# Ten small MLP chunks instead of two, one unit transposed on TensorE instead of four, and early score groups moved from units 26, 62, 98 to 62, 98, 134

## Chip, cores and metric

The kernel runs on one core of one Trainium2 chip. The metric is the device time of one execution in microseconds (us). The median of three runs before the change is 1459.1 us (1457.85 to 1459.69).

## The reference, cut to what matters

Top-32 attention for 8 batches, 8 heads, 576 tokens and head width 64, then a two-layer MLP with a leaky ReLU over all 4608 tokens. Everything is float32.

```
scores = (1/8) * q @ k^T                       # per batch and head, 576 x 576
kth    = 32nd largest score of each row
attn   = softmax of the scores >= kth, others masked out
x      = (attn @ v), heads side by side        # 4608 tokens x 512
h      = x @ w_in                              # 512 -> 2048
out    = max(0.01*h, h) @ w_out                # 2048 -> 512
```

## The kernel before, in words

**Units.** Attention is cut into 144 units (L209 to L216). A whole unit is 128 query rows of two heads (a pair), so four units make 128 tokens complete in all eight heads. 576 is not a multiple of 128, so each batch also has two units that take the 64 rows left over from two pairs each. Even batches have them at the end, odd ones at the start: units 16 to 19, 52 to 55 and so on. Each batch has 18 units.

**A unit's way through the engines.** TensorE makes its scores (`scores`, L218, for two units at once), ScalarE copies them to `s_sb` (L242). VectorE finds the 32 largest of each row (`top_k`, L299; its first instruction for a unit is the TENSOR_TENSOR of L306). GpSimd masks (L324, L325), ScalarE exponentiates (L328) and copies the sums (`ze`, L333), VectorE takes reciprocals (`rz`, L337), ScalarE normalises (L340). Then the weights are transposed: ScalarE splits them into 16-bit halves (L349), SyncE sends these to DRAM (L350) and brings them back transposed (`wT`, L354). The units named in `HASTY` are instead transposed by nine TensorE instructions and two ScalarE copies (L364, L370). TensorE multiplies with v (L393 for two whole units, L405 for left-over units), and ScalarE copies the values to `x` (`keep_values`, L412 to L417).

**The order.** It is written out by hand: the loop over slots at L618 runs `top_k` of unit s in slot s, masks unit s-1, and normalises and transposes unit s-2. In even slots it issues the scores of units s+2 and s+3. The values of a pair of units are issued at the place that `values_at` (L490) gives: for units under 14 in the middle of slot (n|1)+4, later at the end of slot (n|1)+3, and one slot earlier for the units in `HURRIED`. All engines run their own instructions in this order, so an instruction that waits holds back what stands behind it on its engine.

**The MLP.** `CHUNKS` (L54) cuts the 4608 tokens into chunks of 128 or 256. When the values of a chunk's last units have been issued, the chunk is ready. `mlp` (L425) is a generator. Per chunk, 64 matmuls (L436) with the chunk's tokens as moving columns make h, 8 Prelu copies for 256 tokens or 4 for 128 (L442; each covers 512 columns) make `gT`, and 16 matmuls of 512 columns (L448) for each 128 tokens make the output. In the trace each of these float32 matmuls is two records. `x` has two buffers, so chunk c+2 writes where chunk c was read.

**How much MLP in which slot.** `mlp_steps(budget)` is called seven times a slot and issues MLP matmuls until the budget, counted in columns, is used. `slot_budget` (L518) sets it. While at most two chunks have become ready it is `EARLY_SHARE` = 500 per call, 3500 columns a slot. After that, all columns that are ready and not yet issued are spread evenly over the slots up to the next chunk's due slot:

```
        if len(after) >= len(CHUNKS) - EARLY:
            return EARLY_SHARE
        return backlog[0] / ((until + 1 - s) * SLOTS)
```

A chunk of 256 counts as 64 x 256 + 32 x 512 = 32768 columns, one of 128 as 64 x 140 + 16 x 512 = 17152 (`COLUMNS`, L423).

**Early scores.** For a in `KEPT` (L498), the scores of units a, a+1, a+8 and a+9 are made in slots 0 to 5 (`keep_scores`, L277, the matmuls of L286), kept in DRAM, and fetched three slots before they are used (L297). Their slots then have no score matmuls.

Of the kernel before, what the change touches and what calls it, by code (L numbers as in the profile page):

```python
# [20 lines left out]
def kernel(  # L21
# [29 lines left out]
    WCH = 1024  # L51
    LEFT = S % P
    assert D == 64 and S == 576 and HP == 4 and B % 2 == 0 and LEFT == 64
    CHUNKS = [128] * 2 + [256] * 17  # L54
    assert sum(CHUNKS) == B * S
    CHMAX = max(CHUNKS)
    LOADED, LOADED_V = 5, 5
# [260 lines left out]
    def mask(u, i):  # L318
        if i == 0:
            u.nbias = small.tile([P, 2], F32, name="nbias")  # L320
            u.z = small.tile([P, 2], F32, name="z")
            nc.gpsimd.tensor_scalar(u.nbias, u.tops[:, :, 0, 0], -SCALE, None, ALU.mult)
        pen = work.tile([P, S], F32, name="pen", bufs=1)
        nc.gpsimd.tensor_scalar(pen, u.s[i], u.tops[:, i, ROUNDS - 1, 7:8], MASKED, ALU.is_lt, ALU.mult)  # L324
        nc.gpsimd.tensor_tensor(u.s[i], u.s[i], pen, ALU.add)  # L325
# [16 lines left out]
    def transpose(u, between):  # L342


        pairs = u.both.rearrange("p i n -> p (i n)").bitcast(U16).rearrange("p (n h) -> p n h", h=2)
        apart = halves.tile([P, 2, 2 * S], U16, name="apart")
        for h in range(2):
            split = work.tile([P, 2 * S], U16, name="split", bufs=2)
            nc.scalar.copy(split, pairs[:, :, h])  # L349
            nc.sync.dma_start(apart[:, h, :], split)  # L350
            if h == 0:
                between()
        u.wT = work.tile([P, 2 * NKC - 1, P], F32, name="wT", bufs=3)
        nc.sync.dma_start_transpose(out=u.wT.bitcast(U16), in_=apart.rearrange("p h n -> (p h) n"))  # L354

    def transpose_in_haste(u):

        both = u.both.rearrange("p i n -> p (i n)")
        u.parts_T = []
        for c0, c1 in ((0, 8), (8, 2 * NKC - 1)):  # L360
            pt = ps_sc.tile([P, 2, 512], F32, name="wide", bufs=2)
            pt = pt.rearrange("p h (c n) -> p (h c) n", n=P)
            for c in range(c0, c1):
                nc.tensor.transpose(pt[:, c - c0, :], both[:, c * P:(c + 1) * P], ident)  # L364
            u.parts_T.append((c0, c1, pt))

    def keep_transposed(u):
        u.wT = work.tile([P, 2 * NKC - 1, P], F32, name="wT", bufs=3)
        for c0, c1, pt in u.parts_T:
            nc.scalar.copy(u.wT[:, c0:c1, :], pt[:, 0:c1 - c0, :])  # L370

    x_of = {}

    def x_at(token):

        c = 0
        while token >= CHUNKS[c]:
            token -= CHUNKS[c]  # L380
            c += 1
        return c, token
# [29 lines left out]
    def keep_values(pair, po, b, q0):  # L412
        ch, col = x_at(b * S + q0)
        if ch not in x_of:
            x_of[ch] = [xpool.tile([P, CHMAX], F32, name=f"x{c}") for c in range(HP)]
        for side in range(2):
            nc.scalar.copy(x_of[ch][pair % HP + side][:, col:col + po.shape[-1]], po[:, side, :])  # L417
# [7 lines left out]
    def mlp(ch):  # L425

        n = CHUNKS[ch]
        t0 = sum(CHUNKS[:ch])
        x = x_of[ch]
        span = 2 * CHMAX // n  # L430
        for f0 in range(0, NFC, span):
            ph = ps_ml.tile([P, span, n], F32, name="ph", tag="ml")
            for i in range(span):
                f = f0 + i
                for c in range(HP):
                    nc.tensor.matmul(  # L436
                        ph[:, i, :], w_in[c][:, f * P:(f + 1) * P], x[c][:, 0:n],
                        start=(c == 0), stop=(c == HP - 1),
                    )
                    if c == HP - 1 and i + 1 < span or c == 1 and n == CHMAX:  # L440
                        yield COLUMNS[n] * (4 if n < CHMAX else 2)
            nc.scalar.activation(gT[:, f0:f0 + span, 0:n], ph, AF.Prelu, alpha=SLOPE)  # L442
            yield COLUMNS[n] * (4 if n < CHMAX else 2)
        for r0 in range(0, n, P):
            m = min(P, n - r0)
            pz = ps_ml.tile([P, 512], F32, name="pz", tag="ml")
            for f in range(NFC):
                nc.tensor.matmul(  # L448
                    pz[0:m, 0:DMODEL], gT[:, f, r0:r0 + m], w_out[f // 4][:, f % 4, :],
                    start=(f == 0), stop=(f == NFC - 1),  # L450
                )
                if f % 2 and f + 1 < NFC:
                    yield 2 * DMODEL
            o_sb = work.tile([P, DMODEL], F32, name="o_sb", bufs=1)
            nc.scalar.copy(o_sb[0:m], pz[0:m, 0:DMODEL])  # L455
            nc.sync.dma_start(out[t0 + r0:t0 + r0 + m, :], o_sb[0:m])
            yield 2 * DMODEL
# [8 lines left out]
    def mlp_steps(budget):  # L466
        owed[0] += budget
        while owed[0] > 0:
            if running[0] is None:
                if not ready:  # L470
                    owed[0] = 0.0
                    return
                running[0] = mlp(ready.pop(0))
            cost = next(running[0], None)
            if cost is None:
                running[0] = None
            else:
                owed[0] -= cost
                backlog[0] -= cost
# [2 lines left out]

    LAG = 3
    HURRY = 20
    HURRIED = (15, 23, 31)
    HASTY = (14, 15, 23, 31)
    UNHURRIED = 14
    MIDDLE, END = 0, 1

    def values_at(n):  # L490

        if n < UNHURRIED:
            return (n | 1) + LAG + 1, MIDDLE
        return (n | 1) + LAG - ((n | 1) in HURRIED), END

    steps = units

    KEPT = (26, 62, 98)  # L498
    EARLY_SCORES = {0: 4, 1: 2, 2: 1, 3: 2, 4: 1, 5: 2}

    def unit(n):
# [3 lines left out]
    for n, u in enumerate(steps):  # L505
        ch, _ = x_at(u.b * S + u.q0)
# [22 lines left out]
    with tc.manual_schedule():  # L529
        last = {p: n for n, u in enumerate(steps) for p in u.pairs}  # L530
        starts = {p: n for n, u in reversed(list(enumerate(steps))) for p in u.pairs}

        to_keep = [[steps[n] for n in (a, a + 1, a + 8, a + 9)] for a in KEPT]
        early_units = {u for us in to_keep for u in us}
# [60 lines left out]
        def weights_of(u):  # L595
            reciprocals(u)
            normalize(u, 0)
            normalize(u, 1)

        def values(*place):  # L600
            due = [u for n, u in enumerate(steps) if values_at(n) == place]
            if not due:
                return ()
            po = ps_sc.tile([P, 2, 512], F32, name="wide", bufs=2)
            if len(due[0].pairs) == 1:
                weigh_whole(due, po, FULL + [NKC - 1] if place[1] == MIDDLE else
                            [QUARTERS] + FULL if place[0] < HURRY else FULL + [QUARTERS])
                return [(due[0], po[:, :, 0:P])]
            for n, u in enumerate(due):
                weigh_left(u, po[:, :, n * LEFT:(n + 1) * LEFT])  # L610
            return [(u, po[:, :, n * LEFT:(n + 1) * LEFT]) for n, u in enumerate(due)]

        def keep(weighed, *place):
            for u, po in weighed:
                keep_values(u.pairs[0], po, u.b, u.q0)
            attended(*place)

        for s in range(len(steps) + LAG + 1):  # L618
# [9 lines left out]

            at_first = s < HURRY and s - 2 in HURRIED
            if at_first:  # L630
                weights_of(older)
            slot()
            if old:
                mask(old, 0)
                mask(old, 1)
            late = s < HURRY and not {s - 1, s - 2} & set(HURRIED)
            if older and not late and not at_first:
                weights_of(older)
            mlp_steps(budget)
            weighed = values(s, MIDDLE)  # L640
            at_once = s - 2 in HASTY or any(at == (s, MIDDLE) for at, _ in ready_at)
            if at_once:
                keep(weighed, s, MIDDLE)
            slot()
            if older and late:
                weights_of(older)
            if s - 2 in HASTY:
                transpose_in_haste(older)
# [4 lines left out]
            if older:  # L653
                keep_transposed(older) if s - 2 in HASTY else transpose(older, lambda: mlp_steps(budget))
            if not older or s - 2 in HASTY:
                mlp_steps(budget)
# [84 lines left out]
```

## Time and profile before

| | us |
|---|---|
| median of the runs | 1459.1 |
| the profiled execution | 1455.5 |
| its span, first to last instruction | 1453.5 |
| TensorE (PE) matmul busy | 1393.5 |
| VectorE (DVE) busy | 1320.2 |
| ScalarE (ACT) / GpSimd (POOL) busy | 1096.7 / 1099.2 |

The profiled execution lies 3.6 us under the median and has 2 us outside the span. PE means the matmuls, PEld the loads of their stationary operand; the ends of matmuls are modelled, so a PE that is shown busy need not be at its peak. The 40 slices of the page are 36.3 us each; a digit is the busy share in tenths. In a timeline each line has the start, the duration, the engine, the line of the kernel, output<-input, the shape and the number of records, and in brackets the idle time before with what ended it.

"Slot s of DVE" below begins with the first L306 of unit s; "slot s of PE" begins with the first TensorE instruction that the program issues in slot s. The records of PE stand in the program's order, so counting them against the loop tells which slot each belongs to.

### The profile page before, as it was taken

The numbers are of one execution on the slowest core, as the hardware profiler recorded it, in microseconds if no ns is written. First come the engines' busy times: TensorE is split into PE (matmuls) and PEld (weight loads), VectorE is DVE, ScalarE is ACT, GpSimd is POOL, SyncE is SP. The second block draws the span as 40 slices with busy tenths as digits, with TensorE's granted clock in tenths as the row PEclk, the third lists the DMA queues.
The fourth block names the chain that finished last, engine by engine and source line by source line (L and its number), as shares of the span: only waits on it lengthen the run. The fifth ranks groups of instructions, "written<-read, shape, count | busy, mean of one in ns | idle before, by whom it ended". The sixth has DMA issues, their size and how long they took to land.

```text
span 1453.5 us, 26353 instructions
## 1 busy us (share of the span) xinstructions
PE 1393.5 (96%) x9140; PEld 917.4 (63%) x9140; DVE 1320.2 (91%) x3401; ACT 1096.7 (75%) x1976; POOL 1099.2 (76%) x744
## 2 busy tenths in 40 slices
PE   7848999999999999999999999999999999999998
PEld 2326667575756676757676667666666666666674
DVE  7999999999999999999999999999999999999600
ACT  8878777777887787777778778777778777878710
POOL 3288887888888888788888878888888887788600
PEclk9968999999999999999999999999999999999999
DMA  8967542756676645667566644676766654554510
GB/s 331 339 218 229 139 122 83 195 157 164 155 180 172 164 138 156 175 185 179 163 174 170 171 138 134 176 194 163 185 163 185 162 150 120 172 141 133 152 40 15
DMA packets 394998, 239.17 MB, mean 165 GB/s; under 512 B 334576, under 2 KB 336112, under 8 KB 392944
## 3 DMA queue, kind: packets, MB, share of 16 engines
q1 hardware_dynamic: 394864, 237.48, 58.9%
q8 instruction: 72, 1.18, 0.3%
q14 instruction: 62, 0.51, 0.1%
HBM read 55.77 MB, written 99.09 MB: 107 GB/s over the span
## 4 chain that ended last, share of the span: by engine, by line
PE 65%; DVE 24%; DMA 4%; ACT 4%; issue 2%; POOL 0%; DVEq 0%; SPq 0%; ACTq 0%; POOLq 0%
PE ph L436 25%; PE pz L448 25%; DVE tops L311 11%; DVE pairs L314 8%; PE wide L393 8%; PE wide L235 4%; DMA wT<-apart 3%; DVE pairs L306 2%; PE narrow L235 2%; PE wide L405 1%; ACT split L349 1%; ACT s_sb L340 1%; DMA apart<-split 1%; DMA raw<-in_weights_dram 1%; ACT s_sb L328 1%
## 5 line engine op out<-in xcount | busy, mean ns | idle before, releaser
L324 POOL TENSOR_SCALAR pen<-s_sb,tops 128x576 f32<-128x576 f32 x288 | 638.7, 2218 | 194.7 <-DVE tops L311 126.9
L311 DVE MAX8 tops<-pairs 128x8 f32<-128x288 f32 (+1 forms) x1152 | 635.7, 591 | 0.0
L436 PE MATMUL ph<-x,w_in 128*128 128x256 f32 (+1 forms) x2432 | 514.5, 371 | 2.7 <-ACT gT L442 2.7
L448 PE MATMUL pz<-w_out,gT 128*128 128x512 f32 x1152 | 504.4, 594 | 0.0
L436 PEld LDWEIGHTS ph<-x,w_in 128*128 128x128 f32 x2432 | 439.0, 190 | 84.1 <-issue 25.4
L314 DVE MATCH_REPLACE8 pairs<-tops,pairs 128x288 f32<-128x288 f32 (+1 forms) x864 | 460.1, 538 | 0.0
L325 POOL TENSOR_TENSOR s_sb<-s_sb,pen 128x576 f32<-128x576 f32 x288 | 407.7, 1415 | 24.0
L448 PEld LDWEIGHTS pz<-w_out,gT 128*128 128x128 f32 x1152 | 216.5, 190 | 264.9 <-issue 262.1
L349 ACT COPY split<-s_sb 128x1152 uint16<-128x1152 uint16 x280 | 309.5, 1146 | 0.0
L340 ACT ACTIVATE s_sb<-s_sb,rz 128x576 f32<-128x576 f32 x288 | 207.5, 772 | 56.8 <-DVE rz L337 56.6
L328 ACT ACTIVATE s_sb<-s_sb,nbias 128x576 f32<-128x576 f32 x288 | 222.1, 771 | 7.8 <-POOL s_sb L325 7.8
L306 DVE TENSOR_TENSOR pairs<-s_sb 128x576 f32<-128x576 f32 x288 | 214.8, 784 | 9.8 <-DVE tops L311 0.5
L393 PE MATMUL wide<-wT,vt 128*64 128x128 f32 (+1 forms) x2560 | 159.5, 284 | 15.5 <-DMA wT<-apart 7.1
L393 PEld LDWEIGHTS wide<-wT,vt 128*64 128x64 f32 (+1 forms) x2560 | 132.0, 138 | 62.8 <-issue 39.6
L442 ACT ACTIVATE gT<-ph 128x512 f32<-128x512 f32 x144 | 85.4, 593 | 55.9 <-PE ph L436 55.7
L417 ACT COPY x<-wide 128x128 f32<-128x128 f32 (+1 forms) x160 | 32.2, 260 | 114.2 <-PE wide L393 102.2
L242 ACT COPY s_sb<-wide 128x704 f32<-128x704 f32 x130 | 98.2, 755 | 8.4 <-PE wide L235 2.6
L455 ACT COPY o_sb<-pz 128x512 f32<-128x512 f32 x36 | 21.1, 585 | 90.4 <-PE pz L448 90.4
L235 PE MATMUL wide<-kt,qt 64*64 64x352 f32 x704 | 72.6, 475 | 1.0 <-ACT s_sb L257 0.7
L242 ACT COPY s_sb<-narrow 128x448 f32<-128x448 f32 x130 | 63.0, 538 | 0.5
L314 DVE MATCH_VALUE_LOAD pairs<-tops,pairs 128x8 f32 x864 | 62.4, 72 | 0.0
L328 ACT ACTIVATION_READ_ACCUMULATOR s_sb<-s_sb,nbias 128x1 f32 x288 | 55.2, 192 | 0.0
(63 smaller groups left out, 601.6 us busy)
## 6 DMA issues: line engine op xcount, KB each, us to landing
apart<-split SPq DMA_DIRECT2D x280, 288.0 KB, 2.1
raw<-in_weights_dram SPq DMA_DIRECT2D x15, 1024.0 KB, 7.1
vt<-in_vk_dram SPq DMA_DIRECT2D x32, 320.0 KB, 3.6
out_dram<-o_sb SPq DMA_DIRECT2D x36, 256.0 KB, 3.5
kept<-gT SPq DMA_DIRECT2D x12, 576.0 KB, 3.4
s_sb<-kept SPq DMA_DIRECT2D x12, 576.0 KB, 4.9
qt<-in_qT_dram SPq DMA_DIRECT2D x20, 288.0 KB, 3.6
kt<-in_kT_dram SPq DMA_DIRECT2D x20, 288.0 KB, 3.4
```

The source lines that it names most:

```text
L242: nc.scalar.copy(u.both[:, :, k0:k1], to)
L306: nc.vector.tensor_tensor(pairs[:, :, n, :], u.both[:, :, 0:HS], u.both[:, :, HS:S], op)
L311: nc.vector.max(out=u.tops[:, i, r, :], in_=rest[i])
L314: nc.vector.match_replace(out=rest[i], in_to_replace=u.tops[:, i, r, :], in_values=rest[i], imm_value=LOWEST)
L324: nc.gpsimd.tensor_scalar(pen, u.s[i], u.tops[:, i, ROUNDS - 1, 7:8], MASKED, ALU.is_lt, ALU.mult)
L325: nc.gpsimd.tensor_tensor(u.s[i], u.s[i], pen, ALU.add)
L328: nc.scalar.activation(u.s[i], u.s[i], AF.Exp, bias=u.nbias[:, i:i + 1], scale=SCALE, accum_out=u.z[:, i:i + 1])
L340: nc.scalar.activation(u.s[i], u.s[i], AF.Copy, bias=0.0, scale=u.rz[:, i:i + 1])
L349: nc.scalar.copy(split, pairs[:, :, h])
L393: nc.tensor.matmul(po[n * D:(n + 1) * D, side, 0:P], v_of[u.pairs[0]][k, at, side, :], u.wT[k, at + side * NKC if at + 1 < NKC else at, :] ...
L436: nc.tensor.matmul(ph[:, i, :], w_in[c][:, f * P:(f + 1) * P], x[c][:, 0:n], start=(c == 0), stop=(c == HP - 1),)
L448: nc.tensor.matmul(pz[0:m, 0:DMODEL], gT[:, f, r0:r0 + m], w_out[f // 4][:, f % 4, :], start=(f == 0), stop=(f == NFC - 1),)
```

## The change

The first 1280 tokens become ten chunks of 128, and thirteen chunks of 256 follow, where there were two of 128 and seventeen of 256. Only unit 47 is hurried and transposed on TensorE; units 14, 15, 23 and 31 are transposed by DMA, and the values of 15, 23 and 31 (and of their partners 14, 22, 30) are issued one slot later than they were. The twelve units whose scores are made early are now those at 62, 98 and 134. `EARLY`, `EARLY_SHARE` and `COLUMNS` stay. `read` and the assert only state that a chunk was read before its `x` buffer is taken again; they issue nothing.

```
-    CHUNKS = [128] * 2 + [256] * 17
+    CHUNKS = [128] * 10 + [256] * 13
...
-    x_of = {}
+    x_of, read = {}, set()
...
         if ch not in x_of:
+            assert ch < 2 or ch - 2 in read
...
             yield COLUMNS[n] * (4 if n < CHMAX else 2)
+        read.add(ch)
...
-    HURRIED = (15, 23, 31)
-    HASTY = (14, 15, 23, 31)
+    HURRIED = (47,)
+    HASTY = (47,)
...
-    KEPT = (26, 62, 98)
+    KEPT = (62, 98, 134)
```

## The prediction

> **What bounds the kernel now.** I read the page first.
>
> ```profile
> span 1453.5 us, 26353 instructions
> ...
> PE 1393.5 (96%) x9140; PEld 917.4 (63%) x9140; DVE 1320.2 (91%) x3401; ACT 1096.7 (75%) x1976; POOL 1099.2 (76%) x744
> ...
> PE   7848999999999999999999999999999999999998
> ...
> DVE  7999999999999999999999999999999999999600
> ...
> PE 65%; DVE 24%; DMA 4%; ACT 4%; issue 2%; POOL 0%; DVEq 0%; SPq 0%; ACTq 0%; POOLq 0%
> ```
>
> PE and DVE are both nearly full from slice 5 on, and PE alone has the end. So two paces must be compared, stage by stage. Next, the durations, from the groups by form and the PE timelines:
>
> ```profile
> L436 PE MATMUL ph<-x,w_in 128*128 128x256 f32 x2176 | 483.7, 381 | 2.7 <-ACT gT L442 2.7
> ...
> L436 PE MATMUL ph<-x,w_in 128*128 128x128 f32 x256 | 30.8, 281 | 0.0
> ```
>
> ```profile
> 169.65 5.52 PE L436 MATMUL ph<-x,w_in 128*128 128x128 f32 x48
> ```
>
> ```profile
> 1342.59 0.77 PE L235 MATMUL wide<-raw 64*64 64x352 f32 x8
> ...
> 1344.63 14.08 PE L436 MATMUL ph<-x,w_in 128*128 128x256 f32 x64
> ...
> 1375.89 2.35 PE L393 MATMUL wide<-wT,vt 128*64 128x128 f32 x40
> 1378.17 14.00 PE L448 MATMUL pz<-w_out,gT 128*128 128x512 f32 x32
> ...
> 1394.37 27.89 PE L436 MATMUL ph<-x,w_in 128*128 128x256 f32 x128
> 1422.11 27.63 PE L448 MATMUL pz<-w_out,gT 128*128 128x512 f32 x64
> ```
>
> The last two lines are one chunk of 256 alone: 55.4 us. A pair of units costs 1344.63 - 1342.59 = 2.05 us for scores and 1378.17 - 1375.89 = 2.3 us for values (L405 pairs 2.5). Eight steady slots need 55.4 + 4 x 4.35 = 72.8 us of PE. DVE takes 8.87 us a unit where nothing holds it (from its L306 at 194.95 to that at 445.91, 28 units in 251.0, less two stalls of 2.7 together), 71.0 for eight. So PE is the slower one in steady state, by 0.23 us a slot. Last, how they are coupled:
>
> ```profile
> ACT x L417 <- PE wide L393: 102.2, 56, 3.4
> ...
> DVE rz L337 <- ACT ze L333: 33.8, 28, 7.6
> ```
>
> ```profile
> 445.91 1.52 DVE L306 TENSOR_TENSOR pairs<-s_sb 128x576 f32<-128x576 f32 x2
> ```
>
> ```profile
> 448.49 3.83 PE L436 MATMUL ph<-x,w_in 128*128 128x256 f32 x17
> ```
>
> ```profile
> 589.55 1.52 DVE L306 TENSOR_TENSOR pairs<-s_sb 128x576 f32<-128x576 f32 x2
> ```
>
> ```profile
> 595.82 4.37 PE L436 MATMUL ph<-x,w_in 128*128 128x256 f32 x19
> ```
>
> When PE is late, ACT stands at the copies of L417, ze comes late, and DVE stands at rz. These lines are slots 43 and 59, each begun by a chunk: PE is 2.6 and 6.3 us behind DVE. Over all slots the distance never exceeds 6.7. It is small in the other direction too:
>
> ```profile
> 425.89 2.34 PE L393 MATMUL wide<-wT,vt 128*64 128x128 f32 x38 [1.19 <-DMA wT<-apart]
> ```
>
> Slot 40 of DVE began at 419.4: values of a slot can't be weighed before about 6.5 us into it. So PE can neither fall far behind DVE nor run ahead; **work that a stage lacks can't be borrowed from another stage**.
>
> **The change, part by part.** Through slot 14 both programs issue the same MLP: two chunks under EARLY_SHARE. Slot 15 of PE begins at 197.3.
>
> *Slots 15 to 42.* PE's work before: the last 24 records of chunk 1, 24 x 0.432 = 10.4; three chunks of 256, 166.2; 12 score pairs (units 26, 27, 34, 35 were made early) 24.6; 13 values pairs of 2.3 and two of 2.5, 34.9; four transposes by TensorE, 1.3 each, 5.2. Sum 241.3, less than DVE's 28 x 8.87 = 248.4: DVE sets the pace, and PE took 448.5 - 197.3 = 251.2. After: chunks 2 to 8 of 128 fall here. One costs 128 x 5.52/48 = 14.7 plus 32 x 0.432 = 13.8, together 28.5. So 10.4 + 7 x 28.5 + 14 x 2.05 + 34.9 = 273.5. That is over DVE's 248.4: PE sets the pace, at 9.8 us a slot (and about 13.6 in slots 16 to 18, where the backlog of chunks 1 and 2 is due within three slots). With 1 us for waits slot 43 of PE begins at 472, **23.5 later than before, but with 1152 tokens done instead of 1024**. So far nothing is lost: those 128 tokens are worth 27.7.
>
> *Slots 43 to 58.* Only chunk 9, of 128, is ready at the end of slot 42; chunk 10 is ready at the end of slot 49. PE has in slots 43 to 49: 28.5 + 3 score pairs 6.2 + 4 values pairs 9.2 + unit 47's transpose 1.3 = 45.2, where DVE takes 7 x 8.87 = 62.1. In slots 50 to 58 it has 55.4 + 10.3 + 9.6 = 75.3 against 79.8. So DVE paces all 16 slots: 141.9, with 120.5 of PE work. Before, the same slots had two chunks of 256 and took 147.3. DVE begins slot 43 at most 6.7, say 5.5 ahead of PE, at 466.5; slot 59 at 608.4, which is 18.9 after 589.55. PE comes close behind: the last values (6.5 into slot 58), 2.5 + 2.05 for them and the scores, 0.9 of MLP, so slot 59 of PE begins at 599.5 + 12 = 611.5, **15.7 after 595.8**, with the same 1536 tokens done.
>
> *Slots 59 to the end.* Same chunks, due slots and tail. PE starts only 3 us behind DVE, but needs 0.23 a slot more, and is the bound again after some 10 to 20 slots; then waits come back as before. Waits for wT while it is close (slot 62 has one already, 1.5 us at 627.3) may add 1 to 2. KEPT takes the scores of 134, 135, 142 and 143 out of slots 132 and 140: -4.1 at most; where units 98 to 107 lack them now, PE has waits of 0.8 and 1.1, so I take -3.
>
> *Edits that I cost at nothing beside this.* Three more units go through the DMA transpose: 6 splits of 1.15 us on ACT, and on SP 6 stores and 3 transposes, against 6 ACT copies of 0.67 mean. ACT is 75% busy with its idle time in waits for PE; the result lands two slots after the unit, before a PE that is late in slots 15 to 42. Uncovered, each would cost PE the 1.2 us of slot 40. The fetches only move. The values of units 14, 15, 22, 23, 30 and 31 come a slot later but are counted above in either program. Unit 47's nine transposes wait for its normalisation and ahead of them stands nothing urgent, behind them the last matmuls of chunk 9 and the values of 46 and 47; PE is idle in that stage anyway, and if it were not, the 1.05 us that the first of them waited in slot 16 would be the price. Prelus stay 144. A new chunk's first matmuls wait for the x copy behind the values; a run of 256 columns covers it, one of 128 may not: 0 to 0.4 us, eight times, taken as 0.
>
> Sum: +15.7 - 3 + 0.3 = +13. On the profiled execution 1455.5 + 13 = 1468.5; the median is 3.6 higher: **1472**.
>
> *A rule against the row.* The Trainium skill (TensorE: Matmul & The Clock Gate, Back-to-back issue gap) says that in a stream of weight loads and matmuls both set the spacing, about 81 ns at 128 columns and 131 at 512: few columns are dear. Drawn straight between them, 256 columns would take 98, so two chunks of 128 would need 2 x 81/98 = 1.65 times the L436 time of one of 256: 0.65 x 27.7 = 18 us more per replaced chunk, 72 for four. The row says 115 ns against 218 (27.89/128), so 1.06 times, 1.5 us per chunk, 6 for four. Weight loads take 190 ns but overlap; I take the row. Its own ends are 0.112 (the commonest spacing of two records in that stage) and 0.120 (30.8/256, where part ran at a granted clock of 0.82): -3 to +5 us over eight chunks.
>
> **Rivals.**
>
> *A, faster.* PE's work from slot 15 to 146 hardly changes: four swaps +6, transposes -3.9, so +2; yet PE took 1187.8 for 1168 of work, with 20 of waits and loose ends. If early small chunks fill 10 of these (some 8 lie in slots 15 to 44), and the gap of slots 43 to 49 is covered by backlog, the time is 1459 + 2 - 10 = 1451. It decides this way only if DVE can be 17 us or more ahead of PE at slot 43 (62.1 - 45.2), so that PE is still catching up; the trace never shows over 6.7. Chance 6%.
>
> *B, no change.* PE comes out of slots 15 to 42 at 468 (record 0.112), DVE is 6.7 ahead, values are weighed 5 us into a slot as in slot 38, and KEPT brings its 4.1: slot 59 at +8.5, end at +3 to +4. Within 0.2% (2.9 us, about what a measurement of this kernel can tell from no change) or just over: 7%.
>
> *C, a larger loss.* Waits at each chunk's start (+3), 0.120 a record (+5), and PE takes over DVE's whole delay of 18.9 because it waits for wT through slots 59 to 80 and KEPT's gain is lost to such waits: 1459 + 19 + 5 = 1483. For it: the wT waits in the groups' list. Against: in steady state wT lands before PE wants it. Chance 20%.
>
> **How the numbers follow.** Forecast case, 1462 to 1479: 67%; C above it 20%; B 7%, A 6%. Faster 0.06, same 0.07, slower 0.87. Range 1461 to 1482 takes in the record's ends, the chunk starts and half of C.
>
> **What would show it.** In the changed profile: DVE 8.9 a unit up to unit 15, then 9.7 to 9.9 on average up to unit 42, 8.9 without stalls in units 43 to 58; unit 43 begun near 466 and unit 59 near 608; chunk 9's matmuls spread over some 60 us; idle PE of 15 to 20 us between 470 and 610, ended by DMA wT; chunk 12's first L436 (slot 59) near 611; the end about 13 later. Wrong would be: PE full between 470 and 610, unit 59 before 595, or runs of L436 at 128 columns far from 0.115.

## The result, and the profile after

The median after is 1467.65 us (1464.06 to 1470.72, 6 runs) against 1459.3 (1457.76 to 1460.4, 6 runs): ratio 1.0057, 95% interval 1.0041 to 1.0073, or 6 to 11 us slower. The profiled execution took 1467.6, its span 1465.9. The page shows little of it; busy PE has grown by 6.8 us, DVE is as before, and in slices 14 and 15 (476 to 550 us) PE drops to 8:

```profile
span 1465.9 us, 27331 instructions
...
PE 1400.3 (96%) x9623; PEld 940.5 (64%) x9625; DVE 1319.6 (90%) x3401; ACT 1099.1 (75%) x1976; POOL 1098.3 (75%) x744
...
PE   7858999999999889999999999999999999999998
...
DVE  7999996999999999999999999999999999999600
...
PE 75%; DVE 12%; ACT 6%; DMA 6%; issue 1%; POOL 0%; SPq 0%; DVEq 0%; ACTq 0%; POOLq 0%
```

The stage has to be looked at. First the timelines of the kernel after, DVE's and PE's: slots 43 and 59.

```profile
467.13 1.52 DVE L306 TENSOR_TENSOR pairs<-s_sb 128x576 f32<-128x576 f32 x2
```

```profile
473.71 1.05 PE L437 MATMUL ph<-x,w_in 128*128 128x128 f32 x7
```

```profile
611.62 1.52 DVE L306 TENSOR_TENSOR pairs<-s_sb 128x576 f32<-128x576 f32 x2
```

```profile
615.60 1.67 PE L437 MATMUL ph<-x,w_in 128*128 128x256 f32 x7
```

In a table, with the forecast (us; "delay" is against the kernel before):

| | before | forecast | after | delay |
|---|---|---|---|---|
| PE begins slot 43 | 448.5 | 472 | 473.7 | 25.2 |
| DVE begins unit 43 | 445.9 | 466.5 | 467.1 | 21.2 |
| DVE begins unit 59 | 589.55 | 608.4 | 611.6 | 22.1 |
| PE begins slot 59 | 595.8 | 611.5 | 615.6 | 19.8 |
| PE begins slot 146 | 1385.1 | | 1397.4 | 12.3 |

The windows of the kernel after show the same as busy time (columns: length, busy PE, PEld, DVE, ACT, POOL, then granted clock, DMA share and GB/s):

```profile
300.00:467.00 167.00, 164.26 (x1279) 115.38 (x1268) 155.28 (x404) 128.81 (x235) 131.42 (x89) 0.99 0.59 155
467.00:612.00 145.00, 132.08 (x1063) 90.54 (x1066) 141.51 (x370) 112.46 (x211) 120.33 (x81) 0.95 0.57 154
```

Up to unit 43 PE is full and DVE has 12 us of idle time; between units 43 and 59 it is the other way round, PE idle for 13 us. That is less than the 15 to 20 us that the prediction named as a sign. The long waits end with wT, and what follows them is slow:

```profile
485.84 3.95 PE L393 MATMUL wide<-wT,vt 128*64 128x128 f32 x38 [4.36 <-DMA wT<-apart]
```

```profile
521.35 4.31 PE L393 MATMUL wide<-wT,vt 128*64 128x128 f32 x38 [4.44 <-DMA wT<-apart]
```

```profile
503.20:506.60 3.40, 2.71 (x26) 2.71 (x28) 3.37 (x7) 1.28 (x4) 2.62 (x2) 0.50 0.77 256
```

The last line is a window, and its third number from the end is the granted clock, 0.50. At full clock 38 such records take 2.34 us. After these waits they take 3.65 to 4.31, at that clock, which lasts for 3.4 to 6.8 us at a time. The Trainium skill (TensorE: Matmul & The Clock Gate, What's actually happening) has it that a TensorE that was idle for a window of some 3.4 us falls back to half its clock and needs some 3.4 us of work to regain it. The trace agrees with the half clock and the 3.4 us of work, not with the length of the wait: here one of 1.86 us was once enough (values at 335.86: 4.00 us). I had not put this in my sum.

The chain of waits shows what PE waited for. One turn of it:

```profile
485.84 3.95 PE wide L393 x38
489.79 0.65 PE wide L235 x8
...
490.46 0.75 ACT s_sb L242
...
492.83 1.33 ACT s_sb L340 x2
494.17 0.75 ACT s_sb L328 x2
494.92 2.10 ACT split L349 x2
...
497.04 2.11 DMA apart<-split
...
499.28 4.57 DMA wT<-apart
...
503.89 3.65 PE wide L393 x38
```

This is a **loop**: the values wait for wT; the scores stand behind the values on PE; the copies of the scores stand ahead of normalising and splitting on ACT; the split halves go to DRAM and come back as the wT of the next values. One turn is two slots and took 18.05 us here (485.84 to 503.89), next to DVE's 17.74. The slower clock, 1.6 us a turn, is part of it.

### The profile page after: what moved, and what is told of

Its sections match the earlier page's. It is cut to its first block, busy times and chain, and to the rows that moved or that the text cites. A ratio compares the mean times of both kernels' runs of the same rounds, so it can differ in the third digit from the quotient of the medians.

```text
span 1465.9 us, 27331 instructions
## 1 busy us (share of the span) xinstructions
PE 1400.3 (96%) x9623; PEld 940.5 (64%) x9625; DVE 1319.6 (90%) x3401; ACT 1099.1 (75%) x1976; POOL 1098.3 (75%) x744
## 4 chain that ended last, share of the span: by engine, by line
PE 75%; DVE 12%; ACT 6%; DMA 6%; issue 1%; POOL 0%; SPq 0%; DVEq 0%; ACTq 0%; POOLq 0%
PE pz L450 29%; PE ph L437 27%; PE wide L393 10%; PE wide L235 4%; DVE tops L311 4%; DMA wT<-apart 4%; DVE pairs L314 3%; PE narrow L235 3%; ACT split L349 2%; ACT s_sb L340 1%; DMA apart<-split 1%; ACT s_sb L242 1%; DVE pairs L306 1%; ACT s_sb L328 1%; PE wide L405 1%
## 5 line engine op out<-in xcount | busy, mean ns | idle before, releaser
L324 POOL TENSOR_SCALAR pen<-s_sb,tops 128x576 f32<-128x576 f32 x288 | 638.3, 2216 | 208.3 <-DVE tops L311 129.4
L437 PEld LDWEIGHTS ph<-x,w_in 128*128 128x128 f32 x2944 | 458.5, 191 | 70.7 <-issue 28.1
L325 POOL TENSOR_TENSOR s_sb<-s_sb,pen 128x576 f32<-128x576 f32 x288 | 407.3, 1414 | 24.0
L349 ACT COPY split<-s_sb 128x1152 uint16<-128x1152 uint16 x286 | 316.8, 1147 | 0.0
L393 PE MATMUL wide<-wT,vt 128*64 128x128 f32 (+1 forms) x2560 | 167.8, 290 | 24.7 <-DMA wT<-apart 17.4
L393 PEld LDWEIGHTS wide<-wT,vt 128*64 128x64 f32 (+1 forms) x2560 | 138.7, 143 | 71.5 <-issue 38.4
L337 DVE RECIPROCAL rz<-ze 128x2 f32<-128x2 f32 x144 | 22.1, 153 | 47.1 <-ACT ze L333 46.8
```

The source lines that it names most:

```text
L393: nc.tensor.matmul(po[n * D:(n + 1) * D, side, 0:P], v_of[u.pairs[0]][k, at, side, :], u.wT[k, at + side * NKC if at + 1 < NKC else at, :] ...
L437: nc.tensor.matmul(ph[:, i, :], w_in[c][:, f * P:(f + 1) * P], x[c][:, 0:n], start=(c == 0), stop=(c == HP - 1),)
```

## Experiments

Ratios are to the kernel before on the same chip at the same time; where that was, it took 1463.06, 1458.08 or 1461.84 us. An expected time is meant for a kernel before of 1459.1 us, so the ratio is what to compare. (Times are medians, and a ratio need not be exactly that of two medians.) My theory: PE has too much to do in slots 15 to 42, which delays DVE, and too little in slots 43 to 58, where nothing else can use the time. The rivals: small matmuls are dear; the removed TensorE transposes and hurries cost; the move of the kept groups costs; the step from small to large chunks has a fixed price.

**The parts alone.**

```
-    KEPT = (62, 98, 134)
+    KEPT = (26, 62, 98)          # in the kernel after
```

> The changed kernel with the kept groups back at units 26, 62 and 98. Theory (pace and starvation: TensorE has more to do than VectorE in slots 15 to 42, and too little in slots 43 to 58): two score pairs of 2.05 us leave slots 24 and 32, where TensorE is the bound, so slot 59 comes 4 us earlier; they return to slots 132 and 140, where the changed kernel gained about 2 from their absence. Net -2: 1465.5, ratio to before 1.0045. Rival (the move of the kept groups costs the time): back to 1459 to 1460.

Measured: 1489.4, ratio 1.0173 (1.0158 to 1.0188). Theory and rival were both wrong. Was it the chip? The same edit again, beside the unaltered kernel after:

> The changed kernel once more, unaltered, on the chip of this call, to compare the others with. Ratio to before 1.004 to 1.009.

> The changed kernel with the kept groups at 26, 62 and 98 beside the changed kernel itself on one chip. If its first result (ratio 1.0173) belongs to the kernel: 14 to 20 us above the changed kernel again, with longer waits for wT and a lowered clock in slots 43 to 50. If it belonged to the chip of that call: within 4 us of the changed kernel.

Measured: control 1.0068 (1.0056 to 1.008); kept groups at 26 again 1.0162 (1.0145 to 1.018), 12.6 us above the control by the medians, a little under the 14 to 20 expected. It belongs to the kernel. Slot 43 of PE comes equally early in both (472.3 and 472.0), so the 4 us are not even gained. In the stage with too little work, called the thin stage from here on, the waits for wT are longer (first line control, second kept groups at 26; 465 to 616 us):

```profile
PEld wide L393 <- DMA wT<-apart: 14.9, 5, 5.1
```

```profile
PEld wide L393 <- DMA wT<-apart: 18.6, 5, 7.5
```

The halves take 3.4 us to land in DRAM between 465 and 530 us, against 2.9 in the control (mean of L350), one of them 4.50 us on the chain of waits. The clock is halved for 20 us instead of 17, and again for 6.8 us at 724.6. But this is the smaller part of the loss: slot 59 of PE comes 3.1 us after the control's, slot 71 comes 8.2 after, slot 146 14.9 (in the profiled executions). A wait of 2.84 us and the half clock at 724.6, neither of them in the control, account for the step before slot 71. Why the stores land later, and where the rest comes from, is open. Moving the kept groups away from unit 26 was worth some 12 us to this change; it was not a cost.

```
-    KEPT = (26, 62, 98)
+    KEPT = (62, 98, 134)         # in the kernel before
```

> The kernel before with only the kept groups moved to 62, 98 and 134. Theory: TensorE's work in slots 15 to 42 grows from 241.3 to 245.4 us, still under VectorE's 248.4, so 0 to +2 there, and -2 to -3 at the end: 1457 to 1459. Rival (the move of the kept groups costs the time): 1464 or more.

Measured: 1460.88, ratio 0.9987 (0.9979 to 0.9995). By the ratio 1.9 us less, as expected. The part before slot 59 was not: its slot 24 of PE begins with that of the profile before (278.5 and 278.4), its slot 43 comes 4.3 us later and its slot 59 (599.9) 4.1 later, where 0 to 2 were expected. That is the weight of the two score pairs put back into slots 24 and 32, as if PE set the pace there and not DVE; the two profiles are from different chips, so a part may be the chip's.

```
-    HURRIED = (15, 23, 31)
-    HASTY = (14, 15, 23, 31)
+    HURRIED = ()
+    HASTY = ()                   # in the kernel before
```

> The kernel before with no unit hurried and none transposed on TensorE. Theory: TensorE loses 5.2 us of work in slots 16 to 33, chunks 2 to 4 come due a slot later, and the stage stays near VectorE's pace: slot 43 of TensorE within 3 us of 448.5, total 1457 to 1461. Rival (the removed TensorE transposes and hurries are what costs): 1464 to 1470.

Measured: 1464.96, ratio 1.0021 (1.0012 to 1.003), 1.9 us more by the medians, 3 by the ratio. The theory allowed 2, the rival began at 5. But slot 43 came at 455.5 instead of within 3 us of 448.5: chunk 2 came due a slot later, and PE stood idle for 13.6 us in slots 15 to 18. So hurrying was worth 2 to 3 us to the kernel with two small chunks; it is not the loss of 8.

**Where the step stands.**

```
-    CHUNKS = [128] * 10 + [256] * 13
+    CHUNKS = [128] * 6 + [256] * 15      # HURRIED and HASTY (31,), kernel after
```

> The changed kernel with six chunks of 128 and fifteen of 256 (unit 31 hurried and transposed on TensorE instead of 47). Theory: TensorE is over VectorE's pace only in slots 16 to 26, and the thin stage is slots 27 to 42; unit 43 begins about 456 instead of 467.1, and slot 59 of TensorE about 606 instead of 615.6: total 1459 to 1463. Rival (the step from small to large chunks costs a fixed idle time of TensorE of some 13 us, wherever it stands): 1466 to 1469. Rival (the small matmuls are dear): half of the change's loss, 1463.5, with TensorE full throughout.

Measured: 1472.1, ratio 1.0070 (1.0057 to 1.0082), like the control. The theory's total was wrong, the rival's right. In the trace the thin stage has moved to slots 27 to 34, with 13.7 us of idle PE and the clock halved three times. PE begins slot 59 at 611.7, 4.8 before the control, not 10, and slot 146 only 1.2 before it. So the idle time of the step is the larger part and was the same in both places tried; the length of the overloaded stage is the smaller.

```
-    CHUNKS = [128] * 10 + [256] * 13
+    CHUNKS = [128] * 36                  # no unit hurried or hasty, kernel after
...
-    CHMAX = max(CHUNKS)
+    CHMAX = 256                          # so a Prelu still covers 512 columns
```

> The changed kernel with all 36 chunks of 128 tokens, none hurried, none transposed on TensorE. Theory: no step from small to large, so no thin stage; TensorE's work from slot 15 on is 1255 us against 1235 plus 20 idle in the changed kernel, and full throughout: 1465 to 1472. Rival (the small matmuls are dear, 8.4 us for four replaced chunks, so 2.1 each): thirteen more replaced, 1495.

Measured: 1457.64, ratio 0.9998 (0.999 to 1.0006), under the 1465 to 1472 of the theory and far from the rival's 1495. There is no step and no thin stage, and the loss is gone, with 34 small chunks added where the change added 8. Its own sum was right: PE took 1254.5 us from slot 15 to its end, 1255 expected. What I had put too low was the kernel after, whose 1235 us of work came with 31 of waits and slowed matmuls, not 20. This run is not the change without its step and nothing else: PE hardly idles (not at all from slot 43 to 58), slot 59 begins 23.5 us later than before the change and unit 143 28.6 later, and a last chunk of 128, not 256, makes the end shorter. So it speaks of the price of small matmuls, and of the step only in part. Its last chunk alone shows that price:

```profile
1423.49 14.57 PE L437 MATMUL ph<-x,w_in 128*128 128x128 f32 x128
1437.89 13.90 PE L450 MATMUL pz<-w_out,gT 128*128 128x512 f32 x32
```

The 14.57 us of the first line are what the forecast took (14.7). Together with the total this refutes dear small matmuls.

**What sets the pace of the thin stage.** Both kernels with one step of the search left out in units 43 to 58, so that VectorE has less to do:

```
-            if r + 1 < ROUNDS:
+            if r + 1 < ROUNDS and not (r == 2 and 43 <= steps.index(u) < 59):
```

> The changed kernel, but VectorE leaves out the last of the three removal steps of the top-32 search (two 576-wide MATCH_REPLACE8, 1.46 us a unit) in units 43 to 58, so those units' thresholds are not the 32nd largest. Theory (VectorE paces slots 43 to 58): VectorE needs 16 x 7.41 = 118.6 us there instead of 141.9, TensorE 120.5 plus waits, so unit 59 begins 13 to 17 us earlier, and the total falls by 10 to 15, to 1453 to 1457. Rival (TensorE is the bound throughout and the small matmuls cost the time): 0 to -2.

> The kernel before with the same removal steps left out in units 43 to 58. Theory: TensorE has 146 us of work in the 147 us of these slots, so VectorE's 23 us less bring 0 to -2: 1457 to 1459. Rival (VectorE paces this stage in both kernels): -10 or more.

Measured: before 0.9998 (0.999 to 1.0006), as the theory has it; after 1.0075 (1.0059 to 1.0092), no gain at all. That is the rival's number, but not for its reason: PE was idle for 13.0 us in the stage. My "DVE paces these slots" was too simple. PE took 139.2 us from slot 43 to 59 instead of 141.9, though DVE needed only 118.6 and PE 120.5. The loop stood right behind DVE. To cut it, I exchanged scores and values there, alone and together with the shorter search:

```
-            if new and s < HURRY:
+            if new and (s < HURRY or 43 <= s < 59):
                 scores(new)
             keep(values(s, END), s, END)
-            if new and s >= HURRY:
+            if new and s >= HURRY and not 43 <= s < 59:
```

> The changed kernel with only the order of scores and values exchanged in slots 43 to 58. Theory: VectorE's own pace of 8.87 a slot, 141.9 for the stage, stands right behind the loop, so the stage gains 0 to 3 us, and total 0 to 4 under the changed kernel. Rival (the loop and the lowered clock that follows its waits are most of the loss): 8 us, back to the time before.

> The changed kernel with VectorE's last removal step left out in units 43 to 58 (so those units' thresholds are not the 32nd largest), and in slots 43 to 58 the scores of units s+2 and s+3 issued ahead of the slot's values instead of behind them. Theory (in the thin stage a loop sets the pace: values wait for wT, the next scores stand behind them on TensorE, their copies stand ahead of the normalising and splitting on ScalarE, and these lead to the next wT, 17.5 to 18 us for two slots): the loop is cut, and the stage falls from 139 us towards VectorE's 118.6 and TensorE's 120.5, to 122 to 130; total 9 to 16 under the same kernel with values first (ratio to before 0.997 to 1.001 instead of 1.0075). Rival (something else, ScalarE or the DMA queue, holds the stage at 139): no gain.

Measured: scores first 1.0037 (1.0024 to 1.005), 5.1 us under the control by the medians (theory 0 to 4, rival 8). From 478 to 525 us its chain of waits is DVE almost alone. PE still idles for 13.5 us in the stage and its clock is still halved for 13.6, so idle time of PE alone doesn't say what bounds. With the shorter search 1.0045 (1.0031 to 1.0059), about 4 us under that kernel with values first by the ratios, not 9 to 16. PE took 136.9 us for the stage. The chain of waits of this kernel names the next bound:

```profile
577.27 0.63 POOL nbias L322
...
577.97 2.22 POOL pen L324
...
580.28 1.43 POOL s_sb L325
...
581.80 2.21 POOL pen L324
...
584.10 1.62 POOL s_sb L325
...
585.80 0.62 POOL nbias L322
```

GpSimd takes 8.5 us a unit here (577.27 to 585.80), close behind DVE's 8.87, and L324 and L325 make 43% of the chain from 466 to 612 us. That GpSimd is the next bound is read from this chain; no run gave it less work. So DVE (8.87), the loop (9.0) and GpSimd (8.5) lie within 6% of each other, and hurrying DVE, the loop, or both brought the stage from 141.9 us to 136.9 at the best.

**Spreading the work.**

```
-        return backlog[0] / ((until + 1 - s) * SLOTS)
+        return min(backlog[0] / ((until + 1 - s) * SLOTS), 4100 / SLOTS if s < 59 else 1e9)
```

> The changed kernel with one more rule: up to slot 58 the planner hands out at most 4100 columns a slot. The same matmuls, but those over VectorE's pace in slots 16 to 42 are put off into slots 43 to 58: TensorE's work there is 253.9 and 140.9 us against 274 and 120.6, with VectorE's pace 248.4 and 141.9. Theory: slot 43 of TensorE near 453, slot 59 near 596 (as before the change, instead of 615.6), total 1448 to 1454, under the kernel before. Rival (small matmuls are dear): the time of the changed kernel, 1466 to 1468.

Measured: 1454.92, ratio 0.9979 (0.9972 to 0.9987), under the kernel before and, by the ratios, 11 us under the kernel after (a little above the 1448 to 1454 expected). The matmuls, the hurried unit and the kept groups are those of the kernel after; only the slots of the matmuls differ. Its window over about slots 43 to 58 of PE (460.2 to 603.4), to be held against the second one of the kernel after above:

```profile
463.00:605.00 142.00, 140.82 (x1090) 94.32 (x1090) 139.36 (x364) 113.27 (x212) 118.38 (x79) 1.00 0.56 152
```

PE is full where it was idle for 13 us, at full clock. This shows the cause: where the work stands, not what it is. The stage before came out 7 us slower than expected (slot 43 of PE at 460.2, not 453), so slot 59 began at 603.4; between 200 and 300 us and around 380 us it still has short waits and two halved clocks. It is the fastest kernel that I ran.

## Why the prediction was right

Point by point:

- **Slots 15 to 42, PE over DVE's pace:** right. Slot 43 at 473.7 (472). A small matmul cost what the row said: 149.0 us for 1280 records, 0.116, in the groups of the kernel after; 0.115 was taken. The estimate drawn from the rule, that few columns are dear, was 72 us in the place of 6, and nothing of that size appeared.
- **"The distance never exceeds 6.7":** wrong as a general statement. It was read from the kernel before; in slots 18 and 19 of the kernel after, with 13.6 us of PE work a slot in 16 to 18, PE fell 11.0 and 13.5 behind. At slot 43, where the sum used it, it was 6.6. Rival A needed 17.
- **Slots 43 to 58, DVE sets the pace:** the size was near (DVE 144.5 us, forecast 141.9), the reason incomplete. The chain of waits shows that the latency loop set the pace of the first seven slots, at 9.1 us of DVE a unit. Slot 59 of PE came 4.1 later than forecast: DVE began unit 43 0.6 late, took 2.6 longer for the stage, and PE stood 4.0 behind it instead of 3.1. PE was busy for 129.0 us where 120.5 were counted; by my estimate 6.8 of the difference are the 13.6 us at half clock.
- **Slots 59 to the end:** I took -3 for KEPT and +0.3 for waits; measured -7.5 (19.8 to 12.3). About 2 came at slots 132 to 142, less than the 3 I took; of the rest, the waits for wT before the values of slots 75 to 138 gave 4.1 (0.3 us instead of 4.4). The control on another chip gave back less (20.7 to 18.2 at slot 139, against the same profile before), so a part of this is chance.
- **The total:** the profiled execution rose by 12.1 us, forecast 13; the medians by 8.4. That 12.1 lies so near 13 is luck in part: slot 59 came 4.1 later than forecast, and what followed gave back 4.8 more. Of the medians the mis-sized term is the 3.6 us that I added to get from the profiled execution to the median: the profile before was a fast one among its runs, the one after is at its median (1467.64).
- **Rival C** (a larger loss through waits for wT) names a cost that the kept groups at 26 do show in part. Its sum leaves out one of its own terms: with the +3 for the chunks' starts it is 1486, not 1483. (In rival B the terms put slot 59 at about +9, not +8.5.) **Rival A** failed as the point of decision said.

## What to carry to other kernels

When work is made ready earlier, ask what the engine does later, in the stage that used to do it. If the stages are tied together by short queues, work done early at another engine's cost leaves a hole that can't be filled; a planner should hand out at most what the slower engine's pace leaves free and keep the rest for the thin stage. And where several paces lie within 6%, taking work from the one that shows as the bound can bring next to nothing.

## What the runs showed of the hardware

- The granted clock of TensorE fell to 0.50 for 3.4 to 10.2 us after waits of 1.8 to 8.4 us in the middle of the kernels; 38 records of L393 then took 3.65 to 4.31 us instead of 2.34. Not every such wait did it: those of 1.77 and 1.81 us at 638 and 1368 us of the shorter search with scores first, and one of 2.95 us at 500 us of the shorter search with values first, passed at full clock, as did 1.53 us in the kernel before. In the latency loop the slower matmuls are part of the turn.
- The kernel after took up to 6 us more on one chip than on another (1467.65 and 1473.18), while the kernel before differed by 2.5 between these chips (1459.3 and 1461.84).
